# Seventeen stationary columns in the V product, and the order of the score tiles in an attention step

## The chip, the cores and the metric

The kernel runs on one core of one Trainium2 chip. The metric is the device time of one launch in microseconds (us). Three runs of the kernel before gave 1606.13 to 1606.79 us, with a median of 1606.27 us. The profile comes from one further execution under the hardware profiler; all row times below are from that one.

## The reference

The input is x, 2048 tokens of width 512. All of it is float32.

```
xn = layernorm(x)
qkv = xn @ wqkv                        # 32 heads of 16
p = softmax(q @ k.T / 4)               # per head, 2048 x 2048
s = (p @ v) @ wo
g = silu(gelu(xn @ w1 + b1) @ w2 + b2) # inner width 1376
return x + s * g
```

## The kernel before

**Three stages.** In the first, up to about 484 us, the kernel normalizes x, makes q, k and v, computes the gated branch g, and already makes a part of the score tiles from which the row maxima are taken. In the second, up to about 1514 us, it does attention and makes the remaining score tiles beside it. In the third, the attention goes on without score tiles, and the output projection runs in their place. The change touches the second stage and, in one of its halves, the third.

**Units and steps.** The 32 heads form 8 groups of 4, and the 2048 queries 4 chunks of 512, which makes 32 units. A unit has 16 steps, one for each tile of 128 keys, so there are 512 steps. `ORDER` (line 40) writes out what TensorE gets in a step, letter by letter, and the loop at line 948 follows it. In the second stage a step is `TXSTTSTYV`; in the third it is `TTTTV`.

**T** (`t_one`, line 715) makes exp(k q) for one head: one matmul of 512 queries against a stationary tile of 128 keys, then an exp on ScalarE (line 724) which also empties the PSUM tile. The four T of a step are called T1 to T4 here. Their contraction is only 50 rows deep, so they stand in the upper or lower half of the array's rows: T1 and T2 in the half `a = 1`, T3 and T4 in the half `a = 0`. Two matmuls in different halves run side by side. The T tiles lie in four PSUM banks in turn, so each T needs that the exp of the same T in the step before has ended.

**S, X, Y** make the scores once more, transposed, only for the maximum of each row (`s_mm`, line 179; the maximum by VectorE in `s_max`, line 185). S is a whole tile of 512 keys: the first S of a step (S0 here) is in the half `a = 0`, the second (S1) in `a = 1`. X and Y are the two halves of one more tile, 256 keys each: X in the half `a = 0`, Y in `a = 1`. So a step has three score tiles and three maxima, in the order S0, S1, XY. X and Y write to one PSUM bank. So that two halves of the array do not write to it at once, Y waits for an empty instruction on GpSimd (line 217) which waits for X.

**The score banks.** There are three, kept in a ring (`s_tile`, line 91): S0, S1 and X each take the bank that came free first. X keeps its bank out of the ring until Y has been issued. S1 takes the bank of the XY tile of the step before, and so waits for that tile's maximum.

**V** (`pv_step`, line 781) multiplies the exps of the step before with v: four matmuls, one for each head of the unit, side by side in four strips of 32 columns. A head's stationary operand is its 16 columns of v and a column of ones, which gives the softmax denominator: 17 columns (`VW`). The kernel before loads 32 columns, the 17 and 15 of the next head, whose products nobody reads. The operands are full float32, so each of the four matmuls appears as two weight loads and two matmul records. The sum over the 16 key tiles stays in PSUM (`start` for key tile 0) and is then copied out by ScalarE (line 794).

**Behind the loop.** A score unit that has all its maxima goes through `s_end0` (VectorE, GpSimd), `s_end1` (a small transpose on TensorE, line 259) and `s_end2` (a copy and a DMA) into the operand of the T of a later unit. A unit of V goes through `o_move`, `o_den` and `o_div` (DMAs on the SP queue, a reciprocal, a product on GpSimd).

Of the kernel before, what the change touches and what calls it, by code (L numbers as in the profile page):

```python
# [27 lines left out]
GH = 4  # L28
# [3 lines left out]
VW = DH + 1  # L32
# [4 lines left out]
FILL0 = 38  # L37
HB = 4
W2B = 2
ORDER = {0: "TTTTV", 3: "TXSTTSTYV"}  # L40
HC = CH // 2
KB = 3
XB = 6
# [4 lines left out]
def fused(ctx: ExitStack, tc: tile.TileContext, x, wqk, wv, wo, w1, b1, w2, b2, out):  # L48
    nc = tc.nc
# [19 lines left out]
    vsb = keep.tile([P, NT, H * VW + DH], F32, name="vsb")  # L69
# [225 lines left out]
    for i in range(nu):  # L295
        pairs.append(ms[2 * i:2 * i + 2])
        if (i + 1) * len(qs) // nu > i * len(qs) // nu:
            g, c = qs[i * len(qs) // nu]
# [4 lines left out]
    for j in range(len(pairs)):  # L303
        for h in range(2):
# [11 lines left out]
            while nd < ready and n > 0:  # L316
                c, f, k = parts[nd]
# [386 lines left out]
    PT = {}  # L704
# [75 lines left out]
    PV, OS, DN, DR = {}, {}, {}, {}  # L780
    def pv_step(u, k):
        g = u // NCH
        if k == 0:
            PV[u] = ps_v.tile([P, CH], F32, name="pv")
        for j in range(GH):
            h = (g * GH + j) * VW
            nc.tensor.matmul(PV[u][32 * j:32 * j + 32, :], vsb[:, k, h:h + 32], PT[u, k][:, j, :],  # L787
                             start=(k == 0), stop=(k == NT - 1))
        del PT[u, k]
        if k == NT - 1:  # L790
            OS[u] = wb.tile([P, CH], F32, name="os", bufs=1)
            pv = PV.pop(u)
            if u < NU - 1:
                nc.scalar.activation(OS[u], pv, AF.Copy)
            else:
                nc.scalar.activation(OS[u][:, :HC], pv[:, :HC], AF.Copy)
                nc.vector.tensor_copy(OS[u][:, HC:], pv[:, HC:])
# [108 lines left out]
    for u in range(NU):  # L906
        g, c = divmod(u, NCH)
# [36 lines left out]
    for n in range(L + 1):  # L944
        ua, ka = divmod(n, 16)
        want = due(n) - due(n - 1)
        i = 0
        for op in ORDER[want] if n > 1 else ("TTTTV", "TTSTSVT")[n]:
            if op in "SXY":
                s_op(op)  # L950
            elif op == "V":
                if n:
                    pv_step(*divmod(n - 1, 16))
                for _ in range(4):
                    tick()
                flush()
            else:
                if EARLY <= 4 * n + i < 4 * L:
                    t_one(ua, ka, i % 2, 1 - i // 2)
                for f, args in todo.get((n, i), []):  # L960
                    f(*args)
                i += 1
# [56 lines left out]
```

## Time and profile before

| | |
|---|---|
| median of three runs | 1606.27 us |
| span of the profiled execution, first to last instruction | 1603.9 us |
| what lies around the span (median less span) | 2.4 us |
| granted TensorE clock, mean | 1.000 |
| first stage, by the first load of V | 0 to 484 us |
| steps with score tiles (GpSimd instructions of line 217) | 490, from 485.5 to 1513.0 us |

In 500 to 1500 us, every slice of 100 us shows TensorE busy for 100.00 us, VectorE for some 91 and ScalarE for some 98. A matmul that stands waiting for the array or for its weights counts as busy, and so does an activation that overlaps the next one, so these figures do not say by themselves which engine sets the pace.

A row of the timeline gives the start and the length in us, the engine, the source line, the operation, the tile written and the tiles read, the shape, how often, and in brackets how long the engine sat idle before it and which work ended that. PEld is the weight load of TensorE. A row with "x3" is three overlapping or adjoining instructions in one; its length is from the first's start to the last's end.

### The profile page before, as it was taken

What the parts mean: (1) busy time and instruction counts of PE and PEld (TensorE: products, weight loads), DVE (VectorE), ACT (ScalarE), POOL (GpSimd) and SP (SyncE); (2) the same over time, 40 slices, a digit from 0 to 9 for tenths busy, and PEclk for the clock granted to TensorE, in tenths of its full rate; (3) what the DMA queues carried; (4) which work ended last, traced back from release to release, by engine and by line L of the source; (5) the groups of instructions that cost most, each with busy time, mean ns of one, the idle gap of its engine ahead of it and who ended that gap; (6) DMA issues with size and microseconds to landing.
All of it is one profiled execution on the core that took longest, in us unless ns stands there. A gap on an engine that the chain in (4) does not pass through costs nothing.

```text
span 1603.9 us, 32476 instructions
## 1 busy us (share of the span) xinstructions
PE 1593.1 (99%) x12146; PEld 915.7 (57%) x12146; DVE 1383.5 (86%) x2267; ACT 1260.5 (79%) x2524; POOL 377.5 (24%) x398
## 2 busy tenths in 40 slices
PE   8999999999999999999999999999999999999998
PEld 7899989999994444444444444444444444444445
DVE  7489888888989999999999999999999999999734
ACT  4333443434339999999999999999999999999984
POOL 4145565766640001011100200100010000000144
PEclk9999999999999999999999999999999999999999
DMA  6525343454322113111410411221141111110152
GB/s 204 149 59 151 116 136 97 148 145 126 114 89 70 40 30 70 29 36 42 79 32 27 68 42 29 59 42 29 30 70 30 30 29 37 34 29 22 58 200 91
DMA packets 76798, 116.93 MB, mean 73 GB/s; under 512 B 25156, under 2 KB 26436, under 8 KB 75464
## 3 DMA queue, kind: packets, MB, share of 16 engines
q1 hardware_dynamic: 73180, 102.42, 22.4%
q0 software_dynamic: 3264, 12.35, 3.9%
q8 instruction: 96, 1.57, 0.4%
q14 instruction: 62, 0.51, 0.1%
q10 hardware_dynamic: 196, 0.07, 0.0%
HBM read 84.35 MB, written 25.97 MB: 69 GB/s over the span
## 4 chain that ended last, share of the span: by engine, by line
PE 97%; DVE 1%; ACT 0%; DMA 0%; issue 0%; SPq 0%; DVEq 0%; ACTq 0%
PE pv L787 32%; PE ps L179 18%; PE pst L722 16%; PE ps L573 12%; PE pst L573 7%; PE ps L722 5%; PE ps L79 3%; PE pv L573 2%; PE pst L79 1%; DVE slot L74 0%; DMA xt<-in_x 0%; PE pst L259 0%; DVE st L407 0%; PE ps L259 0%; DVE xn L421 0%
## 5 line engine op out<-in xcount | busy, mean ns | idle before, releaser
L185 DVE TENSOR_REDUCE mx<-ps 128x2 f32<-128x512 f32 x2048 | 1299.4, 685 | 153.3 <-PE ps L179 84.9
L724 ACT ACTIVATE slot<-pst 128x512 f32<-128x512 f32 x1533 | 835.1, 612 | 14.2 <-PE pst L722 4.1
L787 PE MATMUL pv<-slot,vsb 128*32 128x512 f32 x4096 | 545.3, 605 | 0.0
L179 PE MATMUL ps<-kt,slot 48*128 48x512 f32 (+1 forms) x1364 | 393.1, 376 | 0.0
L722 PE MATMUL pst<-qt,kt 50*128 50x512 f32 x1149 | 378.1, 430 | 0.5 <-DVE gt L655 0.3
L722 PEld LDWEIGHTS pst<-qt,kt 50*128 50x128 f32 x1149 | 183.0, 184 | 249.6 <-ACT slot L724 246.2
L724 ACT ACTIVATE slot<-ps 128x512 f32<-128x512 f32 x515 | 314.8, 612 | 12.9 <-PE pst L722 8.2
L179 PEld LDWEIGHTS ps<-kt,slot 48*128 48x128 f32 x1364 | 211.3, 184 | 34.2 <-DVE mx L185 23.3
L573 PE MATMUL ps<-slot,w1h 64*128 64x512 f32 x1088 | 220.5, 394 | 0.0
L179 PE MATMUL ps<-kt,qz 48*128 48x512 f32 x512 | 214.9, 420 | 0.0
L179 PE MATMUL ps<-slot,slot 48*128 48x512 f32 (+1 forms) x598 | 172.6, 376 | 0.0
L722 PE MATMUL ps<-qt,kt 50*128 50x512 f32 x387 | 163.0, 423 | 0.0
L573 PEld LDWEIGHTS ps<-slot,w1h 64*128 64x128 f32 x1088 | 152.9, 185 | 6.8 <-ACT junk L587 0.8
L787 PEld LDWEIGHTS pv<-slot,vsb 128*32 128x32 f32 x4096 | 80.6, 108 | 119.8 <-issue 112.0
L573 PE MATMUL ps<-slot,w1l 64*128 64x512 f32 x544 | 143.0, 392 | 0.0
L367 POOL TENSOR_TENSOR hl<-hg,hh 128x512 fp32r<-128x512 f32 x76 | 96.8, 1296 | 131.7 <-ACT hh L366 95.0
L722 PE MATMUL pst<-qt,slot 50*128 50x512 f32 x384 | 119.8, 424 | 0.0
L587 ACT ACTIVATE junk<-ident_r 1x1 f32<-1x1 f32 x92 | 18.0, 196 | 126.4 <-PE pst L573 123.2
L722 PEld LDWEIGHTS ps<-qt,kt 50*128 50x128 f32 x387 | 71.1, 184 | 69.4 <-ACT slot L724 56.5
L179 PEld LDWEIGHTS ps<-kt,qz 48*128 48x128 f32 x512 | 93.7, 183 | 17.4 <-DVE mx L185 0.6
L243 POOL CAST nmh<-nm 128x16 fp32r<-128x16 f32 x32 | 6.3, 197 | 413.1 <-PE pst L722 209.1
L722 PEld LDWEIGHTS pst<-qt,slot 50*128 50x128 f32 x384 | 61.5, 184 | 71.9 <-ACT slot L724 71.6
(150 smaller groups left out, 1744.9 us busy)
## 6 DMA issues: line engine op xcount, KB each, us to landing
raw<-in_w SPq DMA_DIRECT2D x88, 256.0 KB
qk_h<-hh SPq DMA_DIRECT2D x32, 256.0 KB
qk_l<-hl SPq DMA_DIRECT2D x32, 256.0 KB
qt<-qk_h SPq DMA_DIRECT2D x128, 64.0 KB
slot<-qk_h SPq DMA_DIRECT2D x92, 64.0 KB
xt<-in_x SPq DMA_DIRECT2D x16, 256.0 KB
g_d<-gt POOLq DMA_DIRECT2D x16, 256.0 KB, 3.1
qt<-qk_l SPq DMA_DIRECT2D x64, 64.0 KB
```

The source lines that it names most:

```text
L79: nc.tensor.matmul(ps, lhs[a], rhs[b], start=first and n == 0, stop=last and n == 2)
L179: return nc.tensor.matmul(ps[:, c0:c0 + w], QS[u][r, p, qi * P:(qi + 1) * P], kts[u // NCH % KB][p][r, k0:k0 + w], start=True, stop=True).ins
L185: nc.vector.tensor_reduce(MX[u][:, 2 * p:2 * p + 2, qi, ki][:, heads, parts], ps.rearrange("p (n c) -> p n c", c=HC), axis=AX.X, op=OP.max)
L243: nc.gpsimd.tensor_copy(hl[:, 0], nm)
L367: nc.gpsimd.tensor_sub(hl, raw, hh.bitcast(F32))
L573: i = nc.tensor.matmul(ps, lhs[r], rhs[r], start=first, stop=last).ins
L587: i = nc.scalar.activation(junk[:, :1], ident_r[:1, :1].bitcast(F32), AF.Copy).ins
L722: nc.tensor.matmul(ps, kts[g % KB][p][r, k * P:(k + 1) * P], QT[u][r, p, :], start=True, stop=True)
L724: nc.scalar.activation(PT[u, k][:, 2 * p + a, :], ps, AF.Exp, scale=SCALE)
L787: nc.tensor.matmul(PV[u][32 * j:32 * j + 32, :], vsb[:, k, h:h + 32], PT[u, k][:, j, :], start=(k == 0), stop=(k == NT - 1))
```

## The change

In the order of a step, X and the first S change places. In V, the stationary operand has 17 columns instead of 32 for every key tile but the first of a unit; there it keeps 32, so that all 128 rows of the PSUM tile are written once before they are copied out.

```diff
-ORDER = {0: "TTTTV", 3: "TXSTTSTYV"}
+ORDER = {0: "TTTTV", 3: "TSXTTSTYV"}
...
         for j in range(GH):
-            h = (g * GH + j) * VW
-            nc.tensor.matmul(PV[u][32 * j:32 * j + 32, :], vsb[:, k, h:h + 32], PT[u, k][:, j, :],
+            h, w = (g * GH + j) * VW, VW if k else 32
+            nc.tensor.matmul(PV[u][32 * j:32 * j + w, :], vsb[:, k, h:h + w], PT[u, k][:, j, :],
                              start=(k == 0), stop=(k == NT - 1))
```

## The prediction

> **What bounds the kernel now.** I read the profile's page first, then the groups of the second stage, then the timeline of one step.
>
> ```profile
> span 1603.9 us, 32476 instructions
> PE 1593.1 (99%) x12146; PEld 915.7 (57%) x12146; DVE 1383.5 (86%) x2267; ACT 1260.5 (79%) x2524; POOL 377.5 (24%) x398
> PE 97%; DVE 1%; ACT 0%; DMA 0%; issue 0%; SPq 0%; DVEq 0%; ACTq 0%
> ```
>
> By the page the kernel is TensorE from end to end. That needs care, since a matmul that stands in line counts as busy. So next the groups between 500 and 1490 us, with the idle time before them.
>
> ```profile
> L185 DVE TENSOR_REDUCE mx<-ps 128x2 f32<-128x512 f32 x1415 | 891.9, 684 | 87.5 <-PE ps L179 58.2
> L179 PEld LDWEIGHTS ps<-kt,slot 48*128 48x128 f32 x1320 | 204.5, 184 | 32.8 <-DVE mx L185 22.5
> L787 PEld LDWEIGHTS pv<-slot,vsb 128*32 128x32 f32 x3776 | 74.2, 108 | 107.6 <-issue 100.8 <-ACT os L794 6.7
> L794 ACT ACTIVATE os<-pv 128x512 f32<-128x512 f32 x29 | 18.2, 628 | 0.0
> L259 PE MATMUL pst<-ident_r,nmh 128*32 128x128 f32 x17 | 4.2, 247 | 0.0
> L259 PE MATMUL ps<-ident_r,nmh 128*32 128x128 f32 x5 | 1.2, 247 | 0.0
> ```
>
> The loads of the score matmuls do wait for VectorE's maximum. V's 3776 loads, eight a step, make 472 steps in 990 us. The timeline of one step shows which wait counts (the first four rows, from answers for one engine each, are of the step before it).
>
> ```profile
> 1002.49 0.18 PEld L179 LDWEIGHTS ps<-slot,slot 48*128 48x128 f32 x1 [0.15 <-DVE mx L185]
> 1003.03 0.16 PEld L787 LDWEIGHTS pv<-slot,vsb 128*32 128x32 f32 x8 [0.25 <-issue]
> 1002.58 1.89 DVE L185 TENSOR_REDUCE mx<-ps 128x2 f32<-128x512 f32 x3
> 1002.95 1.57 ACT L724 ACTIVATE slot<-pst 128x512 f32<-128x512 f32 x3
> ...
> 1004.03 0.18 PEld L722 LDWEIGHTS ps<-qt,kt 50*128 50x128 f32 x1 [0.84 <-ACT slot L724]
> 1004.03 0.50 PE L722 MATMUL ps<-qt,kt 50*128 50x512 f32 x1
> 1004.03 0.62 PE L179 MATMUL ps<-slot,slot 48*128 48x256 f32 x2
> 1004.26 0.18 PEld L722 LDWEIGHTS pst<-qt,kt 50*128 50x128 f32 x1
> 1004.37 0.52 PE L722 MATMUL pst<-qt,kt 50*128 50x512 f32 x2
> 1004.52 0.18 PEld L179 LDWEIGHTS ps<-slot,slot 48*128 48x128 f32 x1
> 1004.57 0.60 ACT L724 ACTIVATE slot<-ps 128x512 f32<-128x512 f32 x1
> 1004.57 0.18 PEld L722 LDWEIGHTS pst<-qt,kt 50*128 50x128 f32 x1
> 1004.67 0.18 PEld L179 LDWEIGHTS ps<-slot,slot 48*128 48x128 f32 x1
> 1004.69 1.89 DVE L185 TENSOR_REDUCE mx<-ps 128x2 f32<-128x512 f32 x3
> 1004.87 0.28 PE L179 MATMUL ps<-slot,slot 48*128 48x256 f32 x1
> 1005.06 1.57 ACT L724 ACTIVATE slot<-pst 128x512 f32<-128x512 f32 x3
> 1005.07 0.16 PEld L787 LDWEIGHTS pv<-slot,vsb 128*32 128x32 f32 x8 [0.22 <-issue]
> 1006.07 0.18 PEld L722 LDWEIGHTS ps<-qt,kt 50*128 50x128 f32 x1 [0.84 <-ACT slot L724]
> ```
>
> All times below count from T1's load, 1004.03. S1's load is at 0.49 (1004.52), 0.05 after the third maximum of the step before ended (1002.58 + 1.89 = 1004.47). So it waits for the XY bank. That makes a ring over two steps. S0's matmul ends at 0.62; VectorE starts at 0.66, and its three maxima end at 2.55; 0.05 later, at 2.60, S1's load of the *next* step goes. From S1's load to V's are 0.54 to 0.55 (1002.49 to 1003.03, 1004.52 to 1005.07), and from V's load to the T1 after it 1.00 (1005.07 to 1006.07). Sum: 2.60 + 0.54 + 1.00 = 4.14 for two steps. The trace says the same of 14 steps within one unit:
>
> ```profile
> 991.62 0.18 PEld L722 LDWEIGHTS ps<-qt,kt 50*128 50x128 f32 x1 [0.84 <-ACT slot L724]
> 1020.57 0.18 PEld L722 LDWEIGHTS ps<-qt,kt 50*128 50x128 f32 x1 [0.84 <-ACT slot L724]
> L787 PEld LDWEIGHTS pv<-slot,vsb 128*32 128x32 f32 x112 | 2.2, 108 | 3.2 <-issue 3.2
> ```
>
> 28.95 us for 7 pairs is 4.14 a pair. So an ordinary pair is set by VectorE's ring, though VectorE idles in each step and TensorE looks full.
>
> **The second ring.** T4's load waits in the same way for ScalarE: 1004.57 is 0.05 after the exps of the step before ended (1002.95 + 1.57). exp1 starts at 0.54, exp2 to exp4 run from 1.03 to 2.60, and T4's load goes at 2.65. What follows T4 shows where a unit ends, when the copy of L794 has made the exps late:
>
> ```profile
> 1023.56 0.18 PEld L722 LDWEIGHTS pst<-qt,kt 50*128 50x128 f32 x1 [0.21 <-ACT slot L724]
> 1023.99 0.16 PEld L787 LDWEIGHTS pv<-slot,vsb 128*32 128x32 f32 x8 [0.24 <-issue]
> ```
>
> T4's load to V's is 0.43. Sum: 2.65 + 0.43 + 1.00 = 4.08. This ring stands only 0.06 behind the first.
>
> **The change in V.** Two answers on line 787, the first for V's first round of matmuls, the second with the second round, then three matmuls of the step:
>
> ```profile
> L787 PE MATMUL pv<-slot,vsb x4: 617/617/617, 1003.0 to 1003.1; 128*32 128x512 f32 x4
> L787 PE MATMUL pv<-slot,vsb x8: 592/604/617, 1003.0 to 1003.5; 128*32 128x512 f32 x8
> L722 PE MATMUL ps<-qt,kt 50*128 50x512 f32 x1 | 0.5, 498 | 0.0
> L179 PE MATMUL ps<-slot,slot 48*128 48x512 f32 x1 | 0.4, 395 | 0.0
> L179 PE MATMUL ps<-slot,slot 48*128 48x256 f32 x1 | 0.3, 276 | 0.0
> ```
>
> The first round stands 25 ns longer than the second, whose loads ran behind the first. T1, whose 128-column load is open too, has 498 against 395, 103 ns more. That is 0.8 ns a column both times, so 17 columns save 15 x 0.8 = 12 ns a step, once, as only the first round's load is open. No row shows a strip filled in part: the bounds are 0 and 12 ns, and I take 12, since two rows give the same slope. Streams, maxima and copies keep their length.
>
> The Trainium skill speaks against that: the page "TensorE: Matmul & The Clock Gate", section "Architectural detail: the array is 16× 32×32, not 1× 128×128", says that a matmul can begin before its weight load completes. By it V's load could cost nothing now, and the sum would be the first rival's; the 25 ns in these rows do not agree.
>
> **The change of order.** No instruction is added. S0 now streams beside T1 from the start, where X did, and no longer after X's 256 columns. These take 0.12 (395 less 276). So the first maximum can start at 0.54, and VectorE's ring falls to 4.14 - 0.12 - 0.01 = 4.01. VectorE is free by then: the third maximum of the step before ends at 0.44 already now (1004.47). The banks do not hold this up: S0 takes the bank whose maximum came first, X the next, and S1 waits for XY as before.
>
> What gets late is X. It starts at 0.11 + 0.24 = 0.35 instead of 0.11, and T2 behind it, in order, at 0.35 instead of 0.34 (1004.37). Y waits for X by way of GpSimd, and V is queued behind Y on TensorE. Now Y's load is at 0.64 (1004.67) with X's stream over at 0.23, when S0 begins: 0.41 from one to the other. After the change X's stream ends at 0.46, so by this row Y's load is at 0.87 at the latest. The other end: X's record ends at 0.35 + 0.28 = 0.63, and with two signals of 0.05, as between VectorE or ScalarE and TensorE, Y's load goes at 0.73. I take 0.73: in the kernel before, T1's record, issued ahead of X, ends only at 0.50, so most of the 0.41 is X's signal waiting its turn behind T1's.
>
> The Trainium skill, same page, section "The mechanism", has matmuls start and end strictly in program order. By it the wait behind T1 is real and 0.73 holds; without it 0.87, and the sum would be the third rival's. No row here shows X alone.
>
> From Y's load: 0.10 for the load, 0.20 from Y to V's load (1004.87 to 1005.07), then 0.99: V's load at 1.03 to 1.04, the step at 2.03, a pair at 4.06. ScalarE's ring, with V's 0.01 off, is 4.07. So three limits lie within 0.06, and ScalarE's comes last: 0.07 saved a pair.
>
> Behind the loop, the maxima of a score unit end earlier or later by a step or two, so one DMA of row maxima passes a denominator's DMA on SP, and GpSimd's two small casts pass a load or a product. I put that at nothing: the denominators have six steps, some 12 us, till their product. Without that cover a GpSimd piece would hold Y's token.
>
> **The sum.** 490 steps have score tiles. In the window 29 pairs end a unit (L794) and 22 hold L259's transpose, so 472/2 - 51 = 185 are ordinary, and 8 more lie outside: 193 x 0.07 = 13.5 us. The other pairs, 52 in all, are already paced by late exps and get V's 0.012: 0.6. Twenty steps of the third stage get it too: 0.2. In all 14.3: the span goes from 1603.9 to 1589.6 us. The median stands 2.4 above the span (1606.3), so 1592.
>
> **Rivals.** *V's load does not shrink.* The strip is filled as a whole, or the load was never open. For it: no row of a partial strip; against: 0.8 ns a column twice. The pair is 4.08: 193 x 0.06 = 11.6, 1595 us. *TensorE's own pace.* The exps' wait gives way, or X's token comes early. S1 at 0.35 + 0.24, Y at 0.83, V's load 0.20 later and 0.99 make 2.02 a step, 4.04 a pair: 193 x 0.10 = 19.3, with the small terms 20, 1586 us; if the 52 other pairs gained as much, 1582. Against it: T4's load follows the exps by 0.05 in this step. *The token takes VectorE's place.* Y's load at 0.87 puts V's at 0.87 + 0.10 + 0.20 = 1.17 and the step at 2.16, a pair at 4.33: 193 x 0.19 = 37 less 1, 1642 us, slower. It decides from the point where a step passes 2.07, Y's load at 0.78, only 0.05 above my value. For it the 0.41, against it T1's end. *The order does nothing.* The maxima are not the gate after all, or the token eats just what the bank gives: V's 12 ns alone, 193 x 0.012 + 0.8 = 3.1, 1603 us. Against it: the ring's 4.14 is met to the hundredth.
>
> **How the numbers follow.** Forecast 0.52, load 0.12, TensorE's pace 0.13, token 0.13, nothing 0.10. The likeliest gives 1592. The range of 1582 to 1603 runs from TensorE's pace in all pairs to the order that does nothing, and leaves out the slower case. A measurement of this kernel tells 0.2% from no change, some 3.2 us: faster is 0.79, within it 0.08 (most of "nothing"), slower 0.13.
>
> **What would show it.** In the changed profile: an ordinary pair of T1 loads at 4.07; S1's load no longer preceded by an idle time that VectorE ends; T4's load 0.05 behind the exps, in every second step at least; Y's load at 0.73; V's first round 12 ns nearer to its second. A pair of 4.3 with Y's load at 0.87 would make the prediction wrong, one of 4.04 its size.

## The result, and the profile after

The changed kernel takes 1590.25 us (median of four runs, 1589.65 to 1591.26), beside 1606.53 us for the kernel before (four runs now, one of them at 1608.83). The ratio is 0.9901, with a 95% interval of 0.9889 to 0.9914. The forecast was 1592, and the range 1582 to 1603. The profiled execution's span went from 1603.9 to 1587.9 us, 16.0 less.

The top of the page after, and three of its groups between 500 and 1475 us, which correspond to those shown of before:

```profile
span 1587.9 us, 32482 instructions
PE 1577.7 (99%) x12146; PEld 954.9 (60%) x12146; DVE 1382.6 (87%) x2267; ACT 1256.4 (79%) x2524; POOL 378.7 (24%) x398
```
```profile
L185 DVE TENSOR_REDUCE mx<-ps 128x2 f32<-128x512 f32 x1415 | 891.6, 685 | 72.3 <-PE ps L179 28.8 <-PE pst L722 3.1 <-PE ps L722 2.2
L179 PEld LDWEIGHTS ps<-kt,slot 48*128 48x128 f32 x1320 | 217.8, 184 | 1.7
L787 PEld LDWEIGHTS pv<-slot,vsb 128*17 128x17 f32 x3544 | 58.7, 95 | 65.9 <-issue 21.2
```

TensorE is 99% busy as before, and a maximum takes 685 ns beside 684. What is gone is the wait: the loads of the score matmuls stood 32.8 us idle, 22.5 of them for VectorE (500 to 1490 us there), and now 1.7. Two steps of the timeline, in the columns of before, show what sets the pace now:

```profile
1003.16 1.09 ACT L724 ACTIVATE slot<-pst 128x512 f32<-128x512 f32 x2
1003.70 0.18 PEld L722 LDWEIGHTS ps<-qt,kt 50*128 50x128 f32 x1 [0.85 <-ACT slot L724]
1003.71 0.49 PE L179 MATMUL ps<-slot,slot 48*128 48x512 f32 x1
1004.04 0.28 PE L179 MATMUL ps<-slot,slot 48*128 48x256 f32 x1
1004.24 0.60 ACT L724 ACTIVATE slot<-ps 128x512 f32<-128x512 f32 x1
1004.27 3.90 DVE L185 TENSOR_REDUCE mx<-ps 128x2 f32<-128x512 f32 x6 [0.16 <-PE ps L179]
1004.30 0.18 PEld L722 LDWEIGHTS pst<-qt,kt 50*128 50x128 f32 x1
1004.42 0.18 PEld L179 LDWEIGHTS ps<-slot,slot 48*128 48x128 f32 x1
1004.73 1.57 ACT L724 ACTIVATE slot<-pst 128x512 f32<-128x512 f32 x3
1004.74 0.13 PEld L787 LDWEIGHTS pv<-slot,vsb 128*17 128x17 f32 x8
1005.72 0.18 PEld L722 LDWEIGHTS ps<-qt,kt 50*128 50x128 f32 x1 [0.85 <-ACT slot L724]
1006.35 0.18 PEld L722 LDWEIGHTS pst<-qt,kt 50*128 50x128 f32 x1
1006.44 0.18 PEld L179 LDWEIGHTS ps<-slot,slot 48*128 48x128 f32 x1
1006.78 0.13 PEld L787 LDWEIGHTS pv<-slot,vsb 128*17 128x17 f32 x8 [0.16 <-issue]
1007.76 0.18 PEld L722 LDWEIGHTS ps<-qt,kt 50*128 50x128 f32 x1 [0.85 <-ACT slot L724]
```

From T1's load at 1003.70: S0 streams from the start, beside T1, and the first maximum starts at 0.57. X's matmul starts at 0.34, and Y's load goes at 0.72 (1004.42; 0.72 again at 1006.44). The exps end at 2.60 (1004.73 + 1.57 = 1006.30), T4's load of the next step follows 0.05 later at 1006.35, V's load 0.43 behind that, and T1 0.98 behind V's. That is 2.65 + 0.43 + 0.98 = 4.06, and the pair from 1003.70 to 1007.76 is 4.06 long: ScalarE's ring.

V's two rounds of matmuls, 617 and 592 ns in the kernel before:

```profile
L787 PE MATMUL pv<-slot,vsb x4: 603/604/604, 1004.7 to 1004.8; 128*17 128x512 f32 x4
L787 PE MATMUL pv<-slot,vsb x8: 592/598/604, 1004.7 to 1005.2; 128*17 128x512 f32 x8
```

The first round is 13 ns shorter, the second is as it was.

Where the 16.0 us lie: the first loads of step 16 and of step 480, counted from the first step with score tiles, before and then after.

```profile
518.57 0.18 PEld L722 LDWEIGHTS pst<-qt,kt 50*128 50x128 f32 x1 [0.84 <-ACT slot L724]
1493.03 0.18 PEld L722 LDWEIGHTS pst<-qt,kt 50*128 50x128 f32 x1 [0.84 <-ACT slot L724]
```
```profile
517.37 0.18 PEld L722 LDWEIGHTS pst<-qt,kt 50*128 50x128 f32 x1 [0.84 <-ACT slot L724]
1477.49 0.18 PEld L722 LDWEIGHTS pst<-qt,kt 50*128 50x128 f32 x1 [0.84 <-ACT slot L724]
```

These 464 steps went from 974.46 to 960.12 us: 14.3 less. The other 1.7 lie ahead of them (1.2) and behind them (0.5). Of the 1.2, 0.7 are there already when the first stage ends, which the change does not touch: the first load of V comes at 483.8 us before, 483.1 after, and 483.6 in the profile with the order alone. That is a difference between single executions.

### The profile page after: what moved, and what is told of

Same layout as the page of the kernel before. It is cut to its first block, busy times and chain, and to the rows that moved or that the text cites. A ratio compares the mean times of both kernels' runs of the same rounds, so it can differ in the third digit from the quotient of the medians.

```text
span 1587.9 us, 32482 instructions
## 1 busy us (share of the span) xinstructions
PE 1577.7 (99%) x12146; PEld 954.9 (60%) x12146; DVE 1382.6 (87%) x2267; ACT 1256.4 (79%) x2524; POOL 378.7 (24%) x398
## 3 DMA queue, kind: packets, MB, share of 16 engines
q8 instruction: 96, 1.57, 0.4%
## 4 chain that ended last, share of the span: by engine, by line
PE 98%; DVE 1%; DMA 0%; issue 0%; ACT 0%; SPq 0%; DVEq 0%; POOLq 0%; ACTq 0%
PE pv L787 32%; PE pst L722 22%; PE ps L573 13%; PE ps L179 9%; PE pst L573 7%; PE ps L722 7%; PE ps L79 4%; PE pv L573 2%; PE pst L79 1%; DVE slot L74 0%; DMA xt<-in_x 0%; DVE st L407 0%; PE pst L259 0%; PE ps L259 0%; DVE xn L421 0%
## 5 line engine op out<-in xcount | busy, mean ns | idle before, releaser
L787 PE MATMUL pv<-slot,vsb 128*17 128x512 f32 (+1 forms) x4096 | 539.2, 598 | 0.0
L179 PE MATMUL ps<-kt,slot 48*128 48x512 f32 x1364 | 383.6, 370 | 0.1
L722 PEld LDWEIGHTS pst<-qt,kt 50*128 50x128 f32 x1149 | 191.5, 184 | 264.7 <-ACT slot L724 250.6
L179 PEld LDWEIGHTS ps<-kt,slot 48*128 48x128 f32 x1364 | 225.1, 184 | 2.1 <-POOLq L217 0.4
L179 PE MATMUL ps<-slot,slot 48*128 48x512 f32 x598 | 167.8, 368 | 0.0
L787 PEld LDWEIGHTS pv<-slot,vsb 128*17 128x17 f32 (+1 forms) x4096 | 68.7, 96 | 82.8 <-issue 29.4
L722 PEld LDWEIGHTS pst<-qt,slot 50*128 50x128 f32 x384 | 65.9, 184 | 78.0 <-ACT slot L724 73.0
L179 PEld LDWEIGHTS ps<-slot,slot 48*128 48x128 f32 x598 | 98.7, 184 | 1.0
```

The costliest lines, as they stand in the source:

```text
L179: return nc.tensor.matmul(ps[:, c0:c0 + w], QS[u][r, p, qi * P:(qi + 1) * P], kts[u // NCH % KB][p][r, k0:k0 + w], start=True, stop=True).ins
L722: nc.tensor.matmul(ps, kts[g % KB][p][r, k * P:(k + 1) * P], QT[u][r, p, :], start=True, stop=True)
L787: nc.tensor.matmul(PV[u][32 * j:32 * j + w, :], vsb[:, k, h:h + w], PT[u, k][:, j, :], start=(k == 0), stop=(k == NT - 1))
```

## The experiments

Two theories stood against each other. **Rings**: an ordinary pair of steps is set before by VectorE's maxima, and after by ScalarE's exps. **TensorE**: its own work sets the pace, and the waits are incidental. Ratios are to the kernel before on the same chip.

**The two halves of the change, alone.** The first kernel has the new order and 32 columns, the second the old order and 17.

```diff
-ORDER = {0: "TTTTV", 3: "TXSTTSTYV"}
+ORDER = {0: "TTTTV", 3: "TSXTTSTYV"}
```


> The order alone, V with 32 columns as before. Rings (VectorE's maxima set an ordinary pair before, ScalarE's exps after): the pair falls from 4.14 to ScalarE's 4.08 us, 193 pairs x 0.06 = 11.6, about 1595 us against 1606.5. Rival (TensorE's own work sets the pace, the waits on maxima are incidental): a stream of the same columns in another order is worth nothing, 1606 us, pair 4.14.

Measured: 1593.78 us, ratio 0.9927 (0.9914 to 0.9939), 12.0 us less. Two steps in its timeline take 4.07, by T1's loads:

```profile
999.84 0.18 PEld L722 LDWEIGHTS ps<-qt,kt 50*128 50x128 f32 x1 [0.84 <-ACT slot L724]
1003.91 0.18 PEld L722 LDWEIGHTS ps<-qt,kt 50*128 50x128 f32 x1 [0.84 <-ACT slot L724]
```

```diff
-            h = (g * GH + j) * VW
+            h, w = (g * GH + j) * VW, VW if k else 32
...
```


> The 17 columns alone, order as before. Rings: V's load lies once in VectorE's ring of two steps, so a pair loses 12 ns, 4.13 us, 193 x 0.012 + 0.8 = 3 us, about 1603 us. Rival (TensorE's own work sets the pace): 12 ns come off each of 490 steps, 6 us, about 1600 us. If the strip is loaded as a whole: 1606 us.

Measured: 1602.63 us, ratio 0.9981 (0.9972 to 0.9989), 3.1 us less. The loads of the scores still wait for VectorE there, 26.2 us against 22.5 before, though in a window 5 us shorter:

```profile
L179 PEld LDWEIGHTS ps<-kt,slot 48*128 48x128 f32 x1316 | 203.7, 184 | 34.5 <-DVE mx L185 26.2
```

The 464 steps took 971.6 us, 2.9 less than before, which is 12 ns for each of 232 pairs. So V's load counts once in two steps while a ring sets the pace, and the order is worth four times the columns. The two add up to 15 of the 16 us.

**VectorE's work taken down, TensorE's left alone.** Behind the first stage, each maximum reads 448 of 512 scores, in the kernel before and in the changed one. The exp's scale is an eighth, so that nothing overflows; the result is not the reference's.

```diff
-        nc.vector.tensor_reduce(..., ps.rearrange("p (n c) -> p n c", c=HC), axis=AX.X, op=OP.max)
+        nc.vector.tensor_reduce(..., ps.rearrange("p (n c) -> p n c", c=HC)[:, :, :HC if "seen" in prog else 224], axis=AX.X, op=OP.max)
...
-        nc.scalar.activation(PT[u, k][:, 2 * p + a, :], ps, AF.Exp, scale=SCALE)
+        nc.scalar.activation(PT[u, k][:, 2 * p + a, :], ps, AF.Exp, scale=SCALE / 8)
```


> The kernel before with each maximum over 448 of its tile's 512 scores (64 are left out, and the exp's scale is an eighth so that nothing overflows; TensorE's and ScalarE's work is the same). Rings: three maxima a step shorten by some 0.07 us each, VectorE's ring falls from 4.14 to about 3.94, below ScalarE's 4.08, so the pair is 4.08 and the time about 1595 us, with nothing changed on TensorE. Rival (TensorE sets the pace): 1606 us, pair 4.14.

Measured: 1592.43 us, ratio 0.9918 (0.9905 to 0.9932). Two of its groups, and then two steps of 4.08 by T1's loads on the timeline:

```profile
L185 DVE TENSOR_REDUCE mx<-ps 128x2 f32<-128x448 f32 x1413 | 797.2, 618 | 165.9 <-PE ps L179 165.6
L179 PEld LDWEIGHTS ps<-kt,slot 48*128 48x128 f32 x1316 | 216.8, 184 | 1.1
```
```profile
995.13 0.18 PEld L722 LDWEIGHTS ps<-qt,kt 50*128 50x128 f32 x1 [0.84 <-ACT slot L724]
999.21 0.18 PEld L722 LDWEIGHTS ps<-qt,kt 50*128 50x128 f32 x1 [0.84 <-ACT slot L724]
```

A maximum is 66 ns shorter, TensorE's program is the old one, and the kernel gains 13.3 us, 2 more than expected. The TensorE theory falls here: the "99% busy" TensorE had been waiting for VectorE.

> The changed kernel with the same shorter maxima (64 of 512 scores left out, exp's scale an eighth). Rings: VectorE no longer sets the pace, so the pair stays at 4.06 to 4.07 and the time within 1 us of the changed kernel's 1590. If VectorE's ring still binds there: up to 0.2 less a pair, down to 1570 us.

Measured: 1589.81 us, ratio 0.9902 (0.9887 to 0.9917), the same as the changed kernel. After the change, a shorter maximum no longer helps.

**ScalarE's work made longer.** One more activation in each step behind T2's exp, in the kernel before and in the changed one.

```diff
+    pad = keep_r.tile([P, 64], F32, name="pad")
...
         nc.scalar.activation(PT[u, k][:, 2 * p + a, :], ps, AF.Exp, scale=SCALE)
+        if "seen" not in prog and (p, a) == (1, 1):
+            nc.scalar.activation(pad, ident_r[:, :64].bitcast(F32), AF.Copy)
```


> The kernel before with one more activation a step on ScalarE, a copy of 64 columns behind T2's exp, read by nobody; I take 0.1 to 0.15 us of issue for it. Rings: ScalarE's ring grows from 4.08 to 4.18 to 4.23 and takes over from VectorE's 4.14, so about 0.04 to 0.09 a pair, 8 to 17 us, 1614 to 1624 us. Rival (TensorE sets the pace, ScalarE is 98% busy only because activations overlap): 1606 us.

> The changed kernel with the same activation more a step. Rings: ScalarE's ring is the one that binds after the change, so the pair takes the whole 0.1 to 0.15, to 4.17 to 4.22, and the time is 1609 to 1619 us; it ends only some 4 us under the kernel before with the same activation (V's 12 ns a pair), not 16. Rival (TensorE or X's token sets the pace after the change): less than 0.05 a pair, under 1600 us, and the 16 us between the two stay.

Measured: 1629.11 us (ratio 1.0146, 1.0131 to 1.0161) and 1626.11 us (1.0126, 1.0110 to 1.0143). The 16 us between the two kernels shrink to 3.0, as the rings have it: with ScalarE binding in both, the order is worth nothing and V's load is left. Both times lie above what was expected. On ScalarE's timeline, here of the kernel before, the extra activation costs 0.15 of issue, the upper end:

```profile
995.47 0.26 ACT L727 ACTIVATE pad<-ident_r 128x64 f32<-128x64 f32 x1
995.62 1.09 ACT L725 ACTIVATE slot<-pst 128x512 f32<-128x512 f32 x2
```

The ring passes ScalarE's exps in one of its two steps, so a pair pays once, though it has two of the extra activations. And it pays in all 245 pairs with score tiles (490 steps), not in the 193 ordinary ones that I had counted: in the changed kernel an ordinary pair grew by 0.14 (4.06 to 4.20), one with a transpose by 0.11, one at a unit's end by 0.20. 245 x 0.146 = 35.8, and the changed kernel lost 35.9. ScalarE's work sets the pace through the ends of units and the transposes too.

**The token.** X two places further back in the changed kernel.

```diff
-ORDER = {0: "TTTTV", 3: "TSXTTSTYV"}
+ORDER = {0: "TTTTV", 3: "TSTTXSTYV"}
```


> The changed kernel with X moved two places further back, behind T3 (T S T T X S T Y V). Token theory (Y, and with it V, waits for X's end by way of GpSimd): X streams from about 0.59, its record ends at 0.87, Y's load goes at 0.97, V's at 1.27, the step takes 2.26 and a pair 4.52 us, so some 0.45 x 193 = 87 us more, 1677 us. Rival (the token is hidden wherever X stands): pair 4.07, 1590 us.

Measured: 1685.25 us, one run. One step of it:

```profile
996.42 0.18 PEld L722 LDWEIGHTS pst<-qt,kt 50*128 50x128 f32 x1 [0.85 <-ACT slot L724]
997.38 0.18 PEld L179 LDWEIGHTS ps<-kt,slot 48*128 48x128 f32 x1 [0.20 <-POOLq L217]
997.69 0.13 PEld L787 LDWEIGHTS pv<-slot,vsb 128*17 128x17 f32 x8
998.67 0.18 PEld L722 LDWEIGHTS pst<-qt,kt 50*128 50x128 f32 x1 [0.85 <-ACT slot L724]
```

Y's load is at 0.96 and TensorE idles for GpSimd's line 217; the step takes 2.25. The step was expected at 2.26. The time lies 8 us above the expectation, since pairs with a transpose and at a unit's end, which the 193 leave out, become longer too. So the slower rival's mechanism exists, with the expected price of a step, and the new order stays in front of it only because X still starts early enough.

**The next limit.** In the changed kernel, each exp over 448 of 512 queries, the V product unchanged; the result is not the reference's.

```diff
...
-        nc.scalar.activation(PT[u, k][:, 2 * p + a, :], ps, AF.Exp, scale=SCALE)
+        n = 16 * u + k
+        w = 448 if n > 2 else CH
+        nc.scalar.activation(PT[u, k][:, 2 * p + a, :w], ps[:, :w], AF.Exp, scale=SCALE if n > 2 else 0.0)
```
The three PT tiles are allocated once (the part of the edit that is not shown), so that the columns that no exp writes are defined.

> The changed kernel with each exp over 448 of its 512 queries (the other 64 keep ones; TensorE's work is the same). It shows the next limit. Rings: four exps shorten by some 0.05 us each, ScalarE's ring falls by 0.2 to about 3.87; then X's token should hold a pair at 2 x 2.03 = 4.05, so ordinary pairs gain only 0.01 to 0.02, while pairs behind a unit's end gain up to 0.2: 3 + 6 us, about 1581 us. If the token is no limit: TensorE's own 4.02 to 4.04, some 5 us more off.

Measured: 1575.34 us, ratio 0.9812 (0.9797 to 0.9826). Four T1 loads around a unit's end:

```profile
1004.34 0.18 PEld L724 LDWEIGHTS ps<-qt,kt 50*128 50x128 f32 x1 [0.85 <-ACT slot L728]
1006.36 0.18 PEld L724 LDWEIGHTS ps<-qt,kt 50*128 50x128 f32 x1 [0.85 <-ACT slot L728]
1008.40 0.18 PEld L724 LDWEIGHTS ps<-qt,kt 50*128 50x128 f32 x1 [0.84 <-ACT slot L728]
1010.42 0.18 PEld L724 LDWEIGHTS ps<-qt,kt 50*128 50x128 f32 x1 [0.85 <-ACT slot L728]
```

Ordinary steps fall to 2.02, a pair to 4.04: the 0.02 that was expected. The 6 us beyond the expectation are the ends of units: a pair there takes 4.06 instead of 4.48, 12 us in 29 pairs where 6 were expected. What holds the 4.04 is not separated: in the trace S1's load follows a maximum by 0.05, and Y's load follows line 217 by 0.05. The token puts it at 2 x 2.02. VectorE's first maximum now starts at 0.57, not the 0.54 of the prediction, so its ring is 0.57 + 1.89 + 0.05 + 0.54 + 0.98 = 4.03, as near. And the prediction had TensorE's own pace at 4.04.

**A unit's end.** V's first load of the next unit waits for the copy of V's tile, which has to empty V's bank. It did so in the kernel before as well, at all 29 ends of units in the window; its rows at one of them, behind the T1 of 1020.57:

```profile
1020.92 0.63 ACT L794 ACTIVATE os<-pv 128x512 f32<-128x512 f32 x1
```
```profile
1021.61 0.16 PEld L787 LDWEIGHTS pv<-slot,vsb 128*32 128x32 f32 x8 [0.21 <-ACT os L794]
1024.98 0.18 PEld L722 LDWEIGHTS ps<-qt,kt 50*128 50x128 f32 x1 [0.84 <-ACT slot L724]
```

In the changed kernel, first ScalarE's row of the timeline, then TensorE's loads:

```profile
1012.25 0.63 ACT L794 ACTIVATE os<-pv 128x512 f32<-128x512 f32 x1
```
```profile
1011.83 0.18 PEld L722 LDWEIGHTS ps<-qt,kt 50*128 50x128 f32 x1 [0.85 <-ACT slot L724]
1012.93 0.16 PEld L787 LDWEIGHTS pv<-slot,vsb 128*32 128x32 f32 x8 [0.19 <-ACT os L794]
1013.92 0.18 PEld L722 LDWEIGHTS ps<-qt,kt 50*128 50x128 f32 x1 [0.84 <-ACT slot L724]
1016.29 0.18 PEld L722 LDWEIGHTS ps<-qt,kt 50*128 50x128 f32 x1 [0.85 <-ACT slot L724]
```

The step behind it waits for late exps: 4.46 for the two, and 4.41 in the kernel before. From the copy's start to the T1 behind the pair are 4.06 before (1020.92 to 1024.98) and 4.04 after (1012.25 to 1016.29), so this part is no longer than it was. But the copy starts 0.42 behind T1 now, where it started 0.35 behind. Over all ends of units it is 0.43 and 0.40. Two ways were tried to get the copy off ScalarE.

```diff
-            if u < NU - 1:
-                nc.scalar.activation(OS[u], pv, AF.Copy)
-            else:
-                nc.scalar.activation(OS[u][:, :HC], pv[:, :HC], AF.Copy)
-                nc.vector.tensor_copy(OS[u][:, HC:], pv[:, HC:])
+            nc.scalar.activation(OS[u][:, :HC], pv[:, :HC], AF.Copy)
+            nc.vector.tensor_copy(OS[u][:, HC:], pv[:, HC:])
```


> The changed kernel with a unit's copy of V's tile (line 794, on ScalarE 0.63 long) in halves, 256 columns each on ScalarE and on VectorE. Rings: at a unit's end ScalarE's exps start some 0.23 less late, and VectorE's half of some 0.33 us fits almost into its idle time before the first maximum at 0.57. About 0.2 us for each of 30 units, 6 us, 1584 us. Rival (the unit's end is paced by something else than the late exps): 1590 us.

Measured: 1596.32 us, ratio 0.9935 (0.9923 to 0.9948), 6 us *slower* than the changed kernel. The halves do not run side by side; first ScalarE's row, then VectorE's:

```profile
982.90 0.42 ACT L793 ACTIVATE os<-pv 128x256 f32<-128x256 f32 x1
```
```profile
983.35 0.42 DVE L794 COPY os<-pv 128x256 f32<-128x256 f32 x1 [0.45 <-ACT os L793]
```

VectorE's half waits 0.45 for ScalarE's to end, so the maxima behind it are late, and the pair at a unit's end grows from 4.48 to 4.68. The expectation took it for granted that the two halves do not wait for each other. Why VectorE's half has that wait stays open.

```diff
             if u < NU - 1:
-                nc.scalar.activation(OS[u], pv, AF.Copy)
+                nc.vector.tensor_copy(OS[u], pv)
```


> The changed kernel with a unit's copy of V's tile wholly on VectorE. Rings: ScalarE's exps are not late any more, but the first maximum behind the copy starts at about 0.95 instead of 0.57, so VectorE's ring is 4.0 + 0.4 = 4.4 for that pair, against 4.47 now: about 0.1 us for each of 30 units, 3 us, 1587 us, less gain than with the halves. If VectorE's delay has no effect: 4.06 for that pair, 0.4 x 30 = 12 us, 1578 us.

Measured: 1588.56 us (1588.01 to 1588.73), ratio 0.9886 (0.9871 to 0.9901).

```profile
979.17 0.68 DVE L794 COPY os<-pv 128x512 f32<-128x512 f32 x1
979.77 3.76 DVE L185 TENSOR_REDUCE mx<-ps 128x2 f32<-128x512 f32 x6
```
```profile
978.82 0.18 PEld L722 LDWEIGHTS ps<-qt,kt 50*128 50x128 f32 x1 [0.85 <-ACT slot L724]
980.91 0.18 PEld L722 LDWEIGHTS ps<-qt,kt 50*128 50x128 f32 x1 [0.84 <-ACT slot L724]
981.71 0.18 PEld L179 LDWEIGHTS ps<-slot,slot 48*128 48x128 f32 x1 [0.27 <-DVE mx L185]
983.23 0.18 PEld L722 LDWEIGHTS ps<-qt,kt 50*128 50x128 f32 x1 [0.85 <-ACT slot L724]
```

The copy delays the first maximum to 0.95, S1's load of the next step waits for VectorE, and the pair is 4.41 instead of 4.46. This kernel has the lowest time of those that compute the whole reference. Its lead over the changed kernel, 1.7 us, comes from runs on different chips, where the kernel before differed by 0.4, and the intervals of the two ratios overlap. The profiles say the same way: the 464 steps take 958.0 us here and 960.1 in the changed kernel.

> The kernel before with a unit's copy of V's tile wholly on VectorE. Rings: there VectorE's ring binds already, so the copy's delay of the first maximum, about 0.95 instead of 0.66, comes on top: the pair at a unit's end goes from 4.41 to about 4.14 + 0.3 = 4.44, and the edit that gained with the new order gains nothing or loses up to 1 us here, 1606 to 1607 us. Rival (a unit's end is set by the late exps whatever the order): the same 1.5 to 2 us gain as in the changed kernel, 1604 us.

Measured: 1606.41 us, ratio 1.0004 (0.9994 to 1.0013). The same edit is worth nothing where VectorE's ring binds.

## Why the prediction was right

The mean length of a pair of steps in us, by T1's loads, over the same 464 steps of each profile:

| kernel | ordinary (181 pairs) | with a transpose (22) | at a unit's end (29) |
|---|---|---|---|
| before | 4.138 | 4.374 | 4.457 |
| changed | 4.062 | 4.320 | 4.478 |
| order alone | 4.075 | 4.338 | 4.486 |
| columns alone | 4.127 | 4.351 | 4.447 |
| before, shorter maxima | 4.073 | 4.307 | 4.469 |
| before, more ScalarE | 4.214 | 4.443 | 4.691 |
| changed, more ScalarE | 4.202 | 4.434 | 4.680 |
| changed, shorter exps | 4.043 | 4.336 | 4.061 |

**The ring of before** (4.14 from rows, 4.14 in the trace) was the cause. Shorter maxima alone gave 13 us with TensorE's program unchanged, and longer exps made the order worthless.

**The columns.** 12 ns a step were taken, 13 measured; alone they gave 3.1 us where the prediction had 3.1 for them. An ordinary pair is 11 ns shorter by them with the old order and 13 with the new. That a 32-column strip would be loaded as a whole is ruled out.

**The ring of after.** 4.07 was forecast, 4.06 measured, and T4's load stands 0.05 behind the exps in both steps shown. VectorE's ring was put at 4.01 and comes to 4.03 by the rows after, since the first maximum starts at 0.57 and not at 0.54; that decided nothing.

The load of Y was put between 0.73 and 0.87 and taken at 0.73; it is at 0.72. That was the step on which the sign hung, 0.05 from no gain. The rows fit the reason given, that X's signal waits its turn behind T1's. In the kernel before, X's record ended well ahead of T1's, which ran from 0.00 to 0.50:

```profile
1006.07 0.38 PE L179 MATMUL ps<-slot,slot 48*128 48x256 f32 x1
```

X's record ends at 0.38 there, and Y's load is at 0.64, 0.26 later. In the changed kernel X's record ends at 0.62, behind T1's and S0's, and Y's load follows by 0.10. The GpSimd instruction between the two (line 217) comes 0.18 behind the end of X's record in the kernel before and 0.04 behind it in the changed one, so it is X's signal that was late, and not Y that stood in line.

**The sum.** 14.3 us were forecast, 16.0 came in the span, and the first stage's 0.7 of these are luck. The 181 ordinary pairs between step 16 and step 480 gave 13.8: 0.076 a pair and not 0.07, which makes 14.7 for 193 pairs where 13.5 were forecast. The small terms were mis-sized, in both directions. The 22 pairs with a transpose gave 1.2 and not 0.3; why so much stays open. The ends of units lost 0.6 where the prediction had V's 0.012 a pair as a gain. That gain is there behind the copy's start, 4.061 to 4.048 over all ends of units, but the T1 of such a pair now comes 0.03 earlier against the copy, which stands behind the exps on ScalarE; the prediction had not followed that. The 2.4 us between span and median are in part chance too: launch and span of one execution differ by 1.8 (1589.65 less 1587.9), so each of the two profiled executions was some 0.6 quicker than its kernel's median.

## What to carry to other kernels

Where engines hand tiles round through few buffers, add up each ring from a release to the next, over as many steps as it takes, and compare the sums with the measured period; an engine that is "99% busy" with queued matmuls may be waiting all the same. An edit pays only down to the next ring, and that ring's sum is in the same rows: here 4.14 to 4.08, when the first ring alone would have allowed some 4.03. Before an instruction is moved back, find who waits for its end and how much of today's wait is a turn behind others.

## What the runs showed of the hardware

The weight load of a column strip is paid by the columns that it holds, not by the strip: 617 to 604 ns in the first round and 108 to 95 ns in the load's own record, for 17 instead of 32 columns. By the starts of neighbouring instructions, an exp over 512 columns cost 0.477 us of ScalarE's issue, one over 448 cost 0.424, and the extra copy of 64 columns, which reads SBUF and not PSUM, 0.146. So part of the cost does not depend on the columns, and shortening the exps by an eighth gave 0.053 each, not 0.060.
